# Later places for the readers of fresh transfers, and a later start of the first merged second-layer products, in a hand-planned Mamba-2 and expert-mixture kernel

## The chip, the core and the metric

The kernel runs on one core of one Trainium2 chip. The metric is the device time of one execution in microseconds; the time given is the median of several runs. The core has a matrix engine (TensorE, "PE" in the profile, with "PEld" for its weight loads), VectorE ("DVE"), ScalarE ("ACT"), GpSimd ("POOL") and SyncE ("SP"), which here issues nearly all transfers. Each engine takes its own instructions in the order in which the program lists them and waits at semaphores for the others.

## What is computed

Two blocks follow each other, all in float32. The first is a Mamba-2 scan over 4 sequences of 768 positions with 8 heads of 32 channels and a state of 16:

```python
L = np.exp(cum[:, :, :, None] - cum[:, :, None, :]) * causal
CB = np.einsum('bhin,bhjn->bhij', Cc, Bc)
y_intra = np.einsum('bhij,bhjd->bhid', CB * L, xc)
y_inter = np.einsum('bhin,bhnd->bhid', Cc, state) * decay_to_i[:, :, :, None]
y[:, :, sl] = y_intra + y_inter
state = decay_full[:, :, None, None] * state + np.sum(Bx, axis=2)
```

Its output, laid out as 3072 tokens of 256 channels, goes through four dense experts of 1024 hidden units, weighted by normalised domain probabilities:

```python
p = domain_probs / (domain_probs.sum(-1, keepdims=True) + 1e-09)
for e in range(E):
    h = np.maximum(x @ w1[e], 0.0)
    out += p[:, e:e + 1] * (h @ w2[e])
```

## The kernel before

The tokens are cut into 24 chunks of 128. Five blocks of chunk pairs are worked through, three of one scheme (`B`, two pairs) and two of another (`H`, three pairs). Both schemes replace plain products of the expert layers by fewer products of sums: sums of weights (L960, on VectorE or GpSimd), sums of tokens (L979), sums of products (L896, L1045, L1198). One product is a function call with two matmul instructions of 128 by 256 (L869); the profile shows four records for it. The 16 hidden slices of 256 are taken in groups, and a group in a block is a *unit*. A unit's first-layer products end in a gate (L904: relu times the domain probability, on VectorE); its second-layer products continue sums that lie in SBUF between units.

Those sums explain three ScalarE lines. A sum of a second-layer house is kept in a tile `v`: it is *seeded* into a PSUM bank (L883, copy `bank<-v`), products are added to it, and it is copied out again (L1146 for both halves, L1149 for one half). L878 copies an intermediate first-layer sum out of a bank.

The Mamba part of later chunks is woven in between. For each chunk a transfer brings the token data (`xb<-in_xbc_dram`, L430, L432 and L434) and the decays (`ab<-acut_d`). ScalarE then masks the chunk (`ctm<-xb`, L469, two instructions), VectorE scans the decays (L493), TensorE makes the scores (L476), VectorE multiplies them (L793), and TensorE makes outputs and states (L815, L509). Stored sums of weights are written to DRAM once (`w_d<-w`, L965) and reloaded in later blocks (`w<-w_d`, L957). Finished blocks are written out by 32 small stores each (L1253).

The order in which everything stands is made before launch. TensorE's order is written by hand: `put` (L1281) spreads several lists of products evenly over each other, and for every unit the second-layer products of the unit before (`behind`) are spread over its first-layer products (`seq`):

```python
merged = put(behind, seq) if behind else seq
```

For the first unit (`u` is 0) `behind` holds three products that continue one house begun just before the loop (L1340).

All other engines get their order from a planner, `Plan.run` (L185). It walks through time with an assumed cost for each piece of work; an engine takes, among the pieces that are ready, the one that is wanted earliest (`latest`). A piece whose input is a transfer (`kb` is set) counts as ready only `MARGIN`, 2.0 us, after the planned landing (L214). The planner also hands out tiles and banks. Then the pieces are issued in the order of their planned starts, and each engine keeps that order, whenever the inputs really come.

Of the kernel before, what the change touches and what calls it, by code (L numbers as in the profile page):

```python
# [18 lines left out]
HOP = 0.06  # L19
# [6 lines left out]
SOFT = 1  # L26
ROUND = 0, 3, 2, 0, 4
RATE, MARGIN = 330.0, 2.0
AFTER = 1
HOLD = 6.0  # L30
NEAR, WORTH, FIRST = .3, 1.0, 25.0
# [4 lines left out]
BUSY, CALM = 200.0, 1.06  # L36
AHEAD = 3
SOON = 3
EASY = 40.0
HELD = ("x", "w"), (5, 8), (0, 7)  # L40
APART = (0, 7),
# [37 lines left out]
class Plan:  # L79
# [105 lines left out]
    def run(self, line, at, begin):  # L185
# [19 lines left out]
        while todo:  # L205
            e = min(t, key=lambda e: t[e])
            now = t[e]
            best, soon, near = None, None, None
            late = self.late = max(0.0, t["PE"] - line[head].nominal) if head < len(line) else 0.0
            for w in waiting[e]:  # L210
                if w.start is not None or e == "PE" and w.place != head:
                    continue
                ready = max([w.ready, w.after.nominal + late if w.after else 0.0] + [
                    n.end + (MARGIN if n.kb and e != "SP" else -n.lag if n.by == e == "PE" else HOP)  # L214
                    for n in w.needs])
                if len(w.on) > 1 and e == "POOL":
                    if max(ready, now) + w.on[e] > w.latest + late + SLACK or self.backlog(
                            waiting["DVE"], now, t["DVE"], w) < (BACK if now > EASY else 99):
                        continue
                rank = w.latest  # L220
                if e == "DVE" and w.two and self.port > now + 0.05:
                    rank += YIELD
                if best is not None and ready <= now and rank >= best[0]:
                    continue
                when, homes = self.homed(
                    w, max(now, ready, self.port if e == "POOL" and w.port else 0.0))
                if when is None:
                    continue
                if when <= now + 0.02:
                    if best is None or rank < best[0]:  # L230
                        if e == "DVE" and w.two:
                            when = max(when, self.port)
                        best = rank, w, when, homes
                else:
                    if e == "DVE" and when <= now + NEAR and now < FIRST and (near is None or rank < near[0]):
                        near = rank, when
                    if soon is None or when < soon:
                        soon = when
# [16 lines left out]
            _, w, when, homes = best  # L255
# [84 lines left out]
def kernel(  # L340
# [361 lines left out]
    now = 13.2  # L702
# [266 lines left out]
    def token_sums(k):  # L969
        Y, scheme = {}, blocks[k].scheme  # L970

        def get(x):
            return (yT[k, x[1]], lambda v, i=x[0]: v.t[:, i]) if isinstance(x, tuple) else (
                Y[x], lambda v: v.t)

        for r, x, y, sign in scheme.tokens:
            v = Y[r] = value("Y")
            (vx, ax), (vy, ay) = get(x), get(y)
            plan.add({"DVE": D256}, lambda e, v=v, vx=vx, ax=ax, vy=vy, ay=ay, sign=sign: (  # L979
                on(e).tensor_add if sign > 0 else on(e).tensor_sub)(v.t, ax(vx), ay(vy)),  # L980
                two=True, reads=[vx, vy], writes=[v])
        for r in {r for h in scheme.houses for r in h} - {"x", "w"}:
            tokens[k, r] = get(scheme.right.get(r, r))
# [169 lines left out]
    def second(k, groups, houses, held=(), more=()):  # L1153

        seq = []
        for house in houses:
            terms = [
                (r, weights[k, fbs, 2][0][r][0], lambda r=r, fbs=fbs: weights[k, fbs, 2][1](r), T[r])
                for r in house for fbs, T in groups if r in T]
            terms += [t for t in more if t[0] in house]  # L1160
            for only in reversed(house) if house in held and house in APART else (None,):
                if terms:
                    seq += visit(k, house, terms, house in held, only)
        return seq
# [116 lines left out]
    def put(*seqs):  # L1281

        n = [len(s) for s in seqs]
        keys = [((i + (.5 if len(seqs) == 1 else (j + .5) / len(seqs))) / n[j], j, i)
                for j, s in enumerate(seqs) for i in range(n[j])]
        return [seqs[j][i] for _, j, i in sorted(keys)]
# [24 lines left out]
    ones = [(two, {1: begun[two][2]}) for two in twos]  # L1311
    line.extend([*firsts[8:], *second(0, ones[:SOON], [(1, 2)])])
    for c in range(4):
        carry(c)
    units, last_made = [], {}
    for k, b in enumerate(blocks):
        n = E if b.scheme is B else NG
        lead = ROUND[k]
# [8 lines left out]
    def unit_weights(k, groups):  # L1327
        if groups is None:
            plain_weights(k, 0)
        for fbs in groups or ():  # L1330
            for l in (1, 2):
                if fbs in last_made.get(k - 1, ()):
                    weights[k, fbs, l] = weights[k - 1, fbs, l]
                else:
                    operands(k, blocks[k].scheme, fbs, l)
        if groups:
            last_made[k] = groups

    token_sums(0)
    behind = second(0, ones[SOON:], [(1, 2)])  # L1340

    early = [((3 * g + 1, 3 * g + 2, 3 * g + 3), l) for g in range(NG) for l in (1, 2)]
    ending, ends = None, []
    for u, (k, groups) in enumerate(units):
        b = blocks[k]
        of_block = [v for v, (q, _) in enumerate(units) if q == k]
        i = u - of_block[0]
        if AHEAD <= u + 1 < len(units):
            unit_weights(*units[u + 1])
        if i == 0 and k:  # L1350
            token_sums(k)
        if groups is None:
            gates.pop((k, 0), None)
            seq, h = [], {}
            for n in range(b.scheme.pairs):
                s, h[0, n] = plain_first(k, 0, n)
                seq += s
            plain = plain_terms(k, [0], h, b.scheme.plain)
        else:
            made = [threes_first(k, fbs) if b.scheme is H else twos_first(  # L1360
                k, fbs, begun.get(fbs) if k == 0 else None) for fbs in groups]
            seq = put(*[s for s, _ in made])
            right = twos_right if b.scheme is B else threes_right
        merged = put(behind, seq) if behind else seq
        ends.append(merged[-1])
        if ending is not None:
            leave(*ending, due=lambda n=u + AFTER: ends[min(n, len(ends) - 1)])
            ending = None
        for _ in range(EARLY.count(u)):
            operands("early", H, *early.pop(0), merged[0],  # L1370
                     lambda n=u + SOFT: ends[min(n, len(ends) - 1)])
        if groups is None:
            behind = second(k, *held, HELD if k == len(blocks) - 1 else (), plain)
        else:
            held = [(fbs, right(h)) for fbs, (_, h) in zip(groups, made)], b.scheme.houses
            for fbs, T in held[0]:
                if k == 0 and fbs in begun:
                    del T[1]
            plain_next = u + 1 < len(units) and units[u + 1][1] is None
            if plain_next:  # L1380
                held = held[0], LATE
            behind = [] if plain_next else second(k, *held)
        if u == of_block[-1] and k < len(blocks) - 1:
            ending = k, result(k)

        at = {}
        if k < len(blocks) - 1:
            for unit, x, what in PAIRS_AT[len(of_block) if k else 0, blocks[k + 1].scheme.pairs]:
                if unit != i:
                    continue  # L1390
                cs = [blocks[k + 1].first + 2 * int(p) + j for p in what[1:] for j in range(2)]
                mark = len(line)
                if what[0] == "s":
                    for c in cs:
                        fetch(c)
                        decays(c)
                    scores(cs)
                else:
                    outputs(cs)
                    for c in cs:  # L1400
                        carry(c)
                at.setdefault(x, []).extend(line[mark:])
                del line[mark:]
        for x, w in enumerate(merged):
            line.extend(at.get(x, []))
            line.append(w)
# [54 lines left out]
```

## Time and profile before

| what | value |
|---|---|
| median of 3 runs | 624.72 us (624.41 to 624.77) |
| profiled execution | 626.2 us |
| its span, first to last instruction | 624.4 us |
| granted TensorE clock | 0.999 |
| TensorE busy | 616.9 us, 99% |
| VectorE busy | 533.0 us, 85% |
| ScalarE busy | 274.5 us, 44% |
| GpSimd busy | 182.8 us, 29% |
| DMA traffic | 127.44 MB, mean 204 GB/s |

A row of the timeline gives the start, the length, the engine, the line, the operation with output and inputs, and the number of instructions merged into the row; in brackets stands the idle time of the engine just before it and what ended it. A row of the waits names who waited for whom, the total, the number of times and the longest, in microseconds. Times in the trace count from the first instruction.

### The profile page before, as it was taken

What the parts mean: (1) busy time and instruction counts of PE and PEld (TensorE: products, weight loads), DVE (VectorE), ACT (ScalarE), POOL (GpSimd) and SP (SyncE); (2) the same over time, 40 slices, a digit from 0 to 9 for tenths busy, and PEclk for the clock granted to TensorE, in tenths of its full rate; (3) what the DMA queues carried; (4) which work ended last, traced back from release to release, by engine and by line L of the source; (5) the groups of instructions that cost most, each with busy time, mean ns of one, the idle gap of its engine ahead of it and who ended that gap; (6) DMA issues with size and microseconds to landing.
All of it is one profiled execution on the core that took longest, in us unless ns stands there. A gap on an engine that the chain in (4) does not pass through costs nothing.

```text
span 624.4 us, 10261 instructions
## 1 busy us (share of the span) xinstructions
PE 616.9 (99%) x3427; PEld 526.3 (84%) x3427; DVE 533.0 (85%) x879; ACT 274.5 (44%) x582; POOL 182.8 (29%) x208
## 2 busy tenths in 40 slices
PE   9999999999999999999999999999999999999997
PEld 4788888888888888888888788888888888888886
DVE  6999999999968799879788899959797977869684
ACT  5453463423356334336533445445443334555441
POOL 5106775563437575444450001200000000000010
PEclk9999999999999999999999999999999999999999
DMA  7997569884799878389998838635232339643001
GB/s 260 330 336 250 193 226 315 263 265 116 229 354 306 268 246 278 68 287 330 317 333 273 287 69 294 189 115 182 59 101 60 84 66 299 216 137 110 0 2 50
DMA packets 112627, 127.44 MB, mean 204 GB/s; under 512 B 28980, under 2 KB 78144, under 8 KB 112576
## 3 DMA queue, kind: packets, MB, share of 16 engines
q1 hardware_dynamic: 112420, 126.74, 63.0%
q8 instruction: 27, 0.44, 0.3%
q14 instruction: 24, 0.20, 0.1%
q10 hardware_dynamic: 156, 0.06, 0.0%
HBM read 101.87 MB, written 24.89 MB: 203 GB/s over the span
## 4 chain that ended last, share of the span: by engine, by line
PE 96%; ACT 1%; DVE 1%; DMA 1%; issue 0%; SPq 0%; ACTq 0%; DVEq 0%
PE bank L869 89%; PE bank L476 2%; PE bank L509 2%; PE bank L815 1%; PE bank L647 1%; DMA xb<-in_xbc_dram 1%; PE bank L623 0%; DVE v L904 0%; ACT ctm L469 0%; DVE LT L493 0%; DVE v L896 0%; ACT bank L883 0%; ACT v L878 0%; SPq L432 0%; PE bank L1267 0%
## 5 line engine op out<-in xcount | busy, mean ns | idle before, releaser
L869 PE MATMUL bank<-v,w 128*128 128x256 f32 x1816 | 429.7, 380 | 1.0 <-ACT bank L883 0.6
L869 PEld LDWEIGHTS bank<-v,w 128*128 128x128 f32 x1816 | 342.7, 190 | 54.2 <-issue 2.4
L869 PE MATMUL bank<-Y,w 128*128 128x256 f32 x824 | 210.9, 379 | 1.3 <-ACT bank L883 1.3
L896 DVE TENSOR_TENSOR v<-v,v 128x512 f32<-128x512 f32 x262 | 192.0, 763 | 17.5 <-ACT v L878 15.1
L869 PEld LDWEIGHTS bank<-Y,w 128*128 128x128 f32 x824 | 156.2, 190 | 23.6 <-ACT bank L883 1.7
L883 ACT COPY bank<-v 128x512 f32<-128x512 f32 (+1 forms) x201 | 112.4, 571 | 70.6 <-DVE v L896 35.8
L904 DVE SCALAR_TENSOR_TENSOR v<-bank,gate 128x512 f32<-128x512 f32 x172 | 116.1, 682 | 28.2 <-PE bank L869 21.9
L960 POOL TENSOR_TENSOR w<-w,w 128x256 f32<-128x256 f32 x103 | 99.3, 986 | 34.2 <-PE bank L869 18.1
L878 ACT COPY v<-bank 128x512 f32<-128x512 f32 x112 | 65.4, 585 | 96.8 <-PE bank L869 96.3
L1146 ACT COPY v<-bank 128x512 f32<-128x512 f32 x106 | 62.1, 585 | 100.7 <-PE bank L869 99.6
L896 POOL TENSOR_TENSOR v<-v,v 128x512 f32<-128x512 f32 x18 | 25.0, 1396 | 245.4 <-DVE v L896 154.7
L493 DVE TENSOR_TENSOR_SCAN LT<-ab,ident 128x512 f32<-128x512 f32 x42 | 56.2, 1355 | 1.0 <-DMA ab<-acut_d 1.0
L896 DVE TENSOR_TENSOR v<-bank,v 128x512 f32<-128x512 f32 x40 | 27.4, 686 | 8.5 <-PE bank L869 7.6
L503 POOL TENSOR_TENSOR MT<-xb,LT 128x64 f32<-128x64 f32 (+1 forms) x28 | 18.0, 647 | 49.8 <-DVE LT L493 23.4
L778 POOL TENSOR_TENSOR cts<-ctm,dec 128x256 f32<-128x256 f32 x20 | 17.8, 893 | 49.3 <-DVE v L896 14.6
L1198 DVE TENSOR_TENSOR v<-v,v 128x256 f32<-128x256 f32 x54 | 21.9, 442 | 9.2 <-ACT v L1146 9.2
L793 DVE TENSOR_TENSOR MT<-bank,LT 128x512 f32<-128x512 f32 x44 | 27.2, 678 | 1.1 <-PE bank L476 0.8
L1149 ACT COPY v<-bank 128x256 f32<-128x256 f32 x23 | 8.6, 373 | 38.0 <-PE bank L869 37.9
L960 POOL TENSOR_TENSOR w<-w 128x256 f32<-128x256 f32 x15 | 14.2, 951 | 30.8 <-DMA w<-in_w_dram 26.1
L469 ACT ACTIVATE ctm<-xb,tmask 128x128 f32<-128x128 f32 x48 | 16.6, 396 | 11.5 <-DMA xb<-in_xbc_dram 11.2
L1045 DVE TENSOR_TENSOR bank<-bank,v 128x512 f32<-128x512 f32 x24 | 16.6, 692 | 5.7 <-PE bank L869 5.6
L960 DVE TENSOR_TENSOR w<-w,w 128x256 f32<-128x256 f32 x35 | 15.6, 482 | 0.0
(73 smaller groups left out, 203.6 us busy)
## 6 DMA issues: line engine op xcount, KB each, us to landing
w<-w_d SPq DMA_DIRECT2D x138, 256.0 KB
w<-in_w_dram SPq DMA_DIRECT2D x126, 256.0 KB
w_d<-w SPq DMA_DIRECT2D x82, 256.0 KB
ab<-acut_d SPq DMA_DIRECT2D x21, 512.0 KB
w<-in_w_dram SPq DMA_DIRECT2D x42, 128.0 KB
gate<-p_d SPq DMA_DIRECT2D x10, 384.0 KB
xb<-in_xbc_dram SPq DMA_DIRECT2D x17, 192.0 KB
gate<-p_d SPq DMA_DIRECT2D x11, 256.0 KB
```

Source lines behind the costliest of these rows:

```text
L493: nc.vector.tensor_tensor_scan(out=LT.rearrange("p h s -> p (h s)")[:, lo:lo + w], data0=src, data1=ident.rearrange("p h s -> p (h s)")[:, ...
L503: nc.gpsimd.tensor_mul(MT[:, to, P:], b[:, h:h + n], LT[:, to, P - 1:P].to_broadcast([P, n, N]))
L778: plan.add({"POOL": .72}, lambda e: nc.gpsimd.tensor_mul(s["cts"].t, s["ctm"].t, s["dec"].t.unsqueeze(1).to_broadcast([HN, NT, P])), reads ...
L793: nc.vector.tensor_mul(s["MT"].t[:, js, h, 0:P], g, s["LT"].t[:, js, h])
L869: nc.tensor.matmul(out=o, lhsT=w[:, j], rhs=x if half is None else x[:, j], start=(start and j == 0), stop=(j == 1), skip_group_check=True)
L878: act(.5, lambda e: nc.scalar.copy(out=flat(v), in_=bank.t), reads=[bank], writes=[v])
L883: act(.54 if to - lo > FB else .32, lambda e: nc.scalar.copy(out=bank.t[:, lo:to], in_=flat(v)[:, lo:to]), reads=[v], writes=[bank])
L896: plan.add(engines, lambda e: (on(e).tensor_add if sign > 0 else on(e).tensor_sub)(flat(v), whole(x), whole(y)), reads=[x, y], writes=[v], ...
L904: dve(D512, lambda e: nc.vector.scalar_tensor_tensor(out=h.t, in0=whole(x).rearrange("p (j m) -> p j m", j=JJ), scalar=0.0, in1=g.t[:, 2 * ...
L960: plan.add({"POOL": .72} if due else B256, lambda e, r=r, x=x, y=y, sign=sign: (on(e).tensor_add if sign > 0 else on(e).tensor_sub)(view(r ...
L1146: act(.5, lambda e: nc.scalar.copy(out=flat(v), in_=bank.t), reads=[bank], writes=[v])
L1198: plan.add(engines, lambda e: (on(e).tensor_add if sign > 0 else on(e).tensor_sub)(o[1](), x[1](), y[1]()), reads=[v for v in vs if v is n ...
```

## The change

Two things change, both in the making of the order; no instruction's work changes. First, the planner has a second margin. From 100 us of planned time on, a piece on any engine but SyncE that reads a transfer counts as ready 6.0 us after the planned landing, unless its latest start lies less than 8 us ahead; then, and before 100 us, the 2.0 us stay. Second, in the first unit the first two first-layer products are taken out of the spreading and put ahead of it, so that the three merged second-layer products begin later.

```diff
 RATE, MARGIN = 330.0, 2.0
+LEEWAY, SURE = 6.0, 100.0
...
 SOON = 3
+BARE = 2
...
                 ready = max([w.ready, w.after.nominal + late if w.after else 0.0] + [
-                    n.end + (MARGIN if n.kb and e != "SP" else -n.lag if n.by == e == "PE" else HOP)
+                    n.end + ((MARGIN if now < SURE or w.latest + late < now + 8 else LEEWAY) if n.kb and e != "SP" else -n.lag if n.by == e == "PE" else HOP)
                     for n in w.needs])
...
-        merged = put(behind, seq) if behind else seq
+        lead = 0 if u else BARE
+        merged = seq[:lead] + put(behind, seq[lead:]) if behind else seq
```

Since the planner solves the whole order again, tiles, banks and the order on ScalarE, VectorE, GpSimd and SyncE shift throughout; in TensorE's order the three merged products of the first unit stand behind one more product each and nothing else moves. Line numbers after the change are mostly two higher (L871 for L869).

## The prediction

> **What bounds the kernel now.** I read the page first. TensorE is busy for 99% of the span at a granted clock of 0.999, and the chain that ended last is 96% TensorE, so all waits together are worth little; the question is which of TensorE's few waits the change removes, and which it makes.
>
> ```profile
> span 624.4 us, 10261 instructions
> PE 616.9 (99%) x3427; PEld 526.3 (84%) x3427; DVE 533.0 (85%) x879; ACT 274.5 (44%) x582; POOL 182.8 (29%) x208
> PE 96%; ACT 1%; DVE 1%; DMA 1%; issue 0%; SPq 0%; ACTq 0%; DVEq 0%
> 415.73 199.63 PE bank L869 x924
> ```
>
> The last line is from the chain in order of time: 924 matmul records without a break in 199.63 us, so 0.216 us each and 0.864 us for a product of four. That is the yardstick: a product is late by what its start lies behind the last product's start plus 0.864. Second, the waits of TensorE and, in the list of all waits, ScalarE's on fresh transfers:
>
> ```profile
> PE bank L869 <- ACT bank L883: 1.9, 2, 1.3
> ACT ctm L469 <- DMA xb<-in_xbc_dram: 11.2, 6, 2.9
> ```
>
> Third, the timelines at the two waits on the seed copies (L883). At 343 us (SyncE, ScalarE, TensorE):
>
> ```profile
> 339.62 0.84 SPq L432 DMA_DIRECT2D xb<-in_xbc_dram  x2
> 343.92 0.69 ACT L469 ACTIVATE ctm<-xb,tmask 128x128 f32<-128x128 f32 x2 [2.53 <-DMA xb<-in_xbc_dram]
> 344.52 0.56 ACT L1146 COPY v<-bank 128x512 f32<-128x512 f32 x1
> 344.98 0.59 ACT L883 COPY bank<-v 128x512 f32<-128x512 f32 x1
> 343.29 1.03 PE L869 MATMUL bank<-v,w 128*128 128x256 f32 x4
> 345.62 1.13 PE L869 MATMUL bank<-Y,w 128*128 128x256 f32 x4 [1.30 <-ACT bank L883]
> ```
>
> ScalarE takes its instructions in order. It stood 2.53 us at a mask whose token chunk had not landed; behind the mask stood the copy and the seed that TensorE needed. At 30 us:
>
> ```profile
> 30.03 0.37 ACT L1149 COPY v<-bank 128x256 f32<-128x256 f32 x1 [2.56 <-PE bank L869]
> 30.30 1.11 ACT L883 COPY bank<-v 128x512 f32<-128x512 f32 x2
> 29.83 1.03 PE L869 MATMUL bank<-Y,w 128*128 128x256 f32 x4
> 31.47 1.13 PE L869 MATMUL bank<-v,w 128*128 128x256 f32 x4 [0.61 <-ACT bank L883]
> ```
>
> Here no transfer is involved: a merged second-layer product comes one product after the sum that it continues, and the copy out and the seed back take longer than that one product.
>
> **The readers of fresh transfers (first part).** Count and duration of every instruction stay; only the planner's order moves, from 100 us on, by 6.0 instead of 2.0 us after the estimated landing, unless the reader is urgent. In the changed order ten of the twelve chunk masks after 170 us stand 6 to 16 matmul instructions (0.43 us each) further behind their transfer; two near 247 us keep their place. At 343 us the two transfers keep their places in SyncE's queue, the masks come 10 instructions (4.3 us) later, and the copy and the seed now stand ahead of them. The seed's last input is a VectorE L896 that began at 340.72 and took 0.68, so the seed can end near 342.0; its product is due at 343.29 + 0.864 = 344.15. The wait is gone with 2.1 us to spare. Its price: start late by 345.62 - 344.15 = 1.47, and the product behind it started at 346.59, 0.97 later instead of 0.864, so 0.11 for refilling. Together 1.58 us. Late next on ScalarE is the mask itself, still ending near 344.6; behind it stands a copy (L1149) that ran at 345.50 before, so nobody waits. The masks' readers are the scores at 373.5 us, 29 us of cover; without cover this move would cost its 4.3 us.
>
> One row against a rule. Measured: the chain shows 3.77 us from that transfer's last issue, at 340.04, to its landing. The Trainium skill, DMA: Bandwidth & Descriptors, section Anatomy of one DMA, gives about 2.0 us fixed plus bytes over 436 GB/s, fitted for the GpSimd path. My estimate by it is 2.45 us for 192 KB, so 2 us of margin would suffice, the seed would come only some 0.15 us late, this part would be worth about 0.2 us, and the forecast would stand near 624.1. The sum goes by the row.
>
> The other movers: GpSimd's sums of early operands come up to 4 us later. GpSimd was busy 126.5 of the 245 us from 100 to 345 us, and these sums go to DRAM and are reloaded only for the last two blocks, after 338 us, so I cost this at nothing; without that cover a product would wait the 4 us.
>
> **The merged products (second part).** It acts on the first unit alone: three merged products each move behind one more product. TensorE's order changes in nothing else. The first of them is then due at 29.83 + 2 x 0.864 = 31.56, the seed ended at 31.41: the wait is gone with 0.1 us to spare. Price: 31.47 - 30.69 = 0.78, plus refill 32.43 - 31.47 - 0.86 = 0.10, so 0.88 us.
>
> What is late next is VectorE, which hardly idles until 54 us.
>
> ```profile
> 30.81 1.76 DVE L960 TENSOR_TENSOR w<-w,w 128x256 f32<-128x256 f32 x5
> 39.56 1.22 DVE L493 TENSOR_TENSOR_SCAN LT<-ab,ident 128x512 f32<-128x512 f32 x1
> 40.69 0.67 DVE L904 SCALAR_TENSOR_TENSOR v<-bank,gate 128x512 f32<-128x512 f32 x1
> ```
>
> That L904 held TensorE at 41.42; due was 41.14, so 0.28 plus 0.10 of refill. Its counterpart in the changed order stands after 15 weight sums of 0.335 (five in 1.67 us), two combines and four gates of 0.60 (three L904 in 1.86 us) and one scan of 1.14 (L493 to the next): from 30.81 that is 5.03 + 3.60 + 1.14 = 9.77, so 40.58, and its product starts near 40.65 where it was due at 40.20. So the second wait grows from 0.28 to 0.45, and TensorE stands 41.42 - 40.65 = 0.77 us ahead. One scan that stood before this gate now comes after it: VectorE's further work ends 41.37 - 40.58 = 0.79 earlier by the gate but 1.14 later by the scan, 0.35 behind. A combine that took 0.76 there (58.58 to 59.34) goes to GpSimd, so the gate that ended near 59.94 ends near 59.53; its product, 60.14 before, is due at 59.37. With refill this gives back 0.2. I take 0.55 for this part; bounds 0 (VectorE takes all) and 0.88 + 0.38 = 1.26 (both waits go).
>
> **What the trace doesn't show.** The plan is solved again, so the orders of all four other engines change: a third short wait of TensorE, at 112.76 on a score product of VectorE (L793), 0.30 with refill, may go, stay or grow. I take 0.15 off; bounds +0.3 and -0.6 (one more L896 of 0.60 ahead of it). New waits have no row. Between 50 and 615 us the present order has two, of 0.30 and 1.58; I allow one like the smaller, 0.3, bounds 0 and 1.9 (as many as now).
>
> **Sum.** 1.58 + 0.55 + 0.15 - 0.30 = 1.98 us. The profiled execution took 626.2 (span 624.4 and 1.8 around it), 1.5 above the median of the runs, 624.72; it should come to 624.2, and the median to 622.7.
>
> **Rivals.**
>
> No change: the waits go, but the new order brings its own of the present size. 1.58 + 0.55 - 1.88 leaves 0.25, so 624.5; with VectorE giving back nothing and only one wait of 1.58 it is 624.0. For it: 85% VectorE, two places above with 0.1 us to spare, and hundreds of moved instructions. Against it: the present order met 565 us with just two waits, and one of those came from a late transfer, of which there will be fewer. A change that doesn't do what it says (the mask at 343 us stays) would also land here, at 624.72 - 0.55 = 624.2; the changed order speaks against it.
>
> Slower: SyncE's queue. Two reloads of stored sums (L957), wanted by the products at 166.8 and 168.5 us, were issued near 141 to 143 us, ahead of the 32 output stores that fill SyncE from 144.5 to 160.2 us. In the changed order they stand behind these stores, and three stores of early sums (L965) stand among them. Issued at 160.2 as the first reload is now, they land by 164.0: a load issued at 161.24 ended GpSimd's wait at 165.00, 3.8 us. Wanted at 166.1 after 0.7 us of gains; 2.1 us to spare. SyncE's own waits bound what can eat that: L965 on GpSimd at most 2.6 us, on VectorE at most 6.1. At 2.6 the wait is 0.5 and the time 623.2; at 6.1 it is 4.0 plus 0.1, and the time 626.8. It decides beyond 5.3 us of holding: then 3.25 us are lost, and 1.98 less 3.25 is slower by over 0.2%. Against it: the stores also start 8 instructions (3.5 us) earlier in the changed order.
>
> Faster still: both early waits go and nothing new comes, 624.72 - 3.14 - 0.3 = 621.3 with all three terms at their bounds.
>
> **How the numbers follow.** Forecast, with the faster end: 0.60. No change: 0.23. Slower: 0.17. About 0.2% (1.25 us) is what a measurement of this kernel can tell from no change: below 623.47 is faster, above 625.97 slower. The range leaves out 0.05 below and 0.15 above: 621.6 to 626.2. The forecast's own range is 621.6 to 623.5.
>
> **What would show it.** Right: no TensorE wait on L883 near 343 us, the seed ahead of the two masks on ScalarE, the list's wait of ctm on xb far below 11.2 us; no wait at 31 us, one of about 0.45 near 40.6 us; the scores that start at 109.66 start about 0.6 earlier, the last matmul about 2 us. Wrong: a wait of L869 on a DMA near 165 us (the slower rival), waits on L904 between 41 and 62 us that eat the 0.77, or any new wait above 1 us after 100 us.

## The result, and the profile after

The changed kernel takes 623.86 us (median of 20 runs, 623.26 to 624.86) where the kernel before takes 624.98 us on the same chip (median of 20, 623.88 to 626.64). The ratio is 0.998, with a 95% interval of 0.9973 to 0.9987. So it is faster by 1.1 us, 0.2%: just under what I had called the least that can be told, and little more than half of the 2.0 us forecast. (The ranges of times and the ratios in this document leave out three executions, of 647, 1531 and 1666 us, that ran in a slow state.)

The profiled execution took 623.26 us, 2.36 of it outside the span; in the profile before, 1.8 of 626.2 lay outside. The page after, its span, its engines and the engines' shares of the chain that ended last:

```profile
span 620.9 us, 10264 instructions
PE 615.4 (99%) x3427; PEld 526.0 (85%) x3427; DVE 533.5 (86%) x882; ACT 275.5 (44%) x582; POOL 179.1 (29%) x205
PE 97%; DVE 1%; ACT 1%; issue 0%; DVEq 0%
```

The span is 3.5 us shorter, the time only 2.9. DMA has left the chain. The list of waits after has no row of ScalarE's mask on its transfer (11.2 us in six waits before). TensorE's waits in the main products are these three; none is on a seed:

```profile
PE bank L871 <- ACT v L880: 0.3, 1, 0.3
PE bank L871 <- DVE v L906: 0.2, 1, 0.2
PE bank L871 <- DVE MT L795: 0.2, 1, 0.2
```

The timeline after at the two places of the prediction, near 340 us (ScalarE, SyncE, TensorE) and near 30 us (ScalarE, TensorE):

```profile
339.40 0.59 ACT L1148 COPY v<-bank 128x512 f32<-128x512 f32 x1 [2.58 <-PE bank L871]
339.89 0.60 ACT L885 COPY bank<-v 128x512 f32<-128x512 f32 x1
340.41 1.29 ACT L471 ACTIVATE ctm<-xb,tmask 128x128 f32<-128x128 f32 x4
333.92 0.84 SPq L434 DMA_DIRECT2D xb<-in_xbc_dram  x2
342.60 1.03 PE L871 MATMUL bank<-Y,w 128*128 128x256 f32 x4
```

```profile
29.64 1.11 ACT L885 COPY bank<-v 128x512 f32<-128x512 f32 x2
29.18 1.89 PE L871 MATMUL bank<-Y,w 128*128 128x256 f32 x8
30.90 1.04 PE L871 MATMUL bank<-v,w 128*128 128x256 f32 x4
```

The seed stands ahead of the masks and ends 2.1 us before its product starts at 342.60; the four mask instructions run without any wait. That they don't wait has a second cause beside their later place: the last chunk's transfers, in the row at 333.92, were issued 5.7 us earlier than before (339.62), while TensorE was only 1.6 ahead. Near 30 us eight records (two products) follow each other, and the product on the seed follows them with no gap. Two places are new or larger, near 58.7 and 111.5 us:

```profile
57.33 1.28 DVE L906 SCALAR_TENSOR_TENSOR v<-bank,gate 128x512 f32<-128x512 f32 x2
58.66 1.56 PE L871 MATMUL bank<-v,w 128*128 128x256 f32 x6 [0.24 <-DVE v L906]
111.47 1.35 PE L871 MATMUL bank<-v,w 128*128 128x256 f32 x5 [0.21 <-DVE MT L795]
```

**Where the time went.** I subtract each TensorE start before from its counterpart after, and count the refill of about 0.1 us behind a wait with the wait. TensorE is 0.67 us ahead at the first product of the expert layers (start-up: 13.20 against 12.53 us). It gains 0.86 more at 31 us and 0.36 at 41; loses 0.48 at 58.7, gains 0.15 of it back at the scores near 64, loses 0.11 at 80, 0.15 at 111.5 and 0.12 at 131; gains 0.39 at 172 and 1.55 at 343. The 0.39 at 172 is not the change's: a later execution of the kernel before (e11) gains as much there over this first one. The last matmul starts 3.12 us earlier. From there to the end of the span it is 3.75 us, where it was 4.19. But 0.6 us of this comes back outside the span, and this before was among the slowest of its runs and this after the fastest of its own. So the experiments also compare distributions.

### The profile page after: what moved, and what is told of

The parts are those of the page before. It is cut to its first block, busy times and chain, and to the rows that moved or that the text cites. A ratio compares the mean times of both kernels' runs of the same rounds, so it can differ in the third digit from the quotient of the medians.

```text
span 620.9 us, 10264 instructions
## 1 busy us (share of the span) xinstructions
PE 615.4 (99%) x3427; PEld 526.0 (85%) x3427; DVE 533.5 (86%) x882; ACT 275.5 (44%) x582; POOL 179.1 (29%) x205
## 4 chain that ended last, share of the span: by engine, by line
PE 97%; DVE 1%; ACT 1%; issue 0%; DVEq 0%
PE bank L871 91%; PE bank L511 2%; PE bank L478 2%; PE bank L649 1%; PE bank L817 1%; PE bank L625 0%; DVE v L906 0%; DVE w L962 0%; DVE LT L495 0%; DVE MT L795 0%; ACT ctm L471 0%; DVE v L898 0%; PE bank L1269 0%; PE bank L617 0%; ACT A L521 0%
## 5 line engine op out<-in xcount | busy, mean ns | idle before, releaser
L871 PE MATMUL bank<-v,w 128*128 128x256 f32 x1816 | 429.5, 380 | 0.7 <-ACT v L880 0.3
L871 PEld LDWEIGHTS bank<-v,w 128*128 128x128 f32 x1816 | 342.7, 190 | 53.8 <-issue 4.0
L871 PE MATMUL bank<-Y,w 128*128 128x256 f32 x824 | 210.6, 379 | 0.0
L898 DVE TENSOR_TENSOR v<-v,v 128x512 f32<-128x512 f32 x258 | 188.9, 764 | 16.4 <-ACT v L880 15.2
L871 PEld LDWEIGHTS bank<-Y,w 128*128 128x128 f32 x824 | 156.3, 190 | 21.9 <-issue 0.6
L962 POOL TENSOR_TENSOR w<-w,w 128x256 f32<-128x256 f32 x100 | 95.1, 973 | 60.2 <-PE bank L871 23.1
L880 ACT COPY v<-bank 128x512 f32<-128x512 f32 x112 | 65.5, 586 | 95.7 <-PE bank L871 92.3
L898 POOL TENSOR_TENSOR v<-v,v 128x512 f32<-128x512 f32 x22 | 30.3, 1382 | 261.8 <-DVE v L898 157.6
L495 DVE TENSOR_TENSOR_SCAN LT<-ab,ident 128x512 f32<-128x512 f32 x42 | 54.5, 1317 | 0.4 <-DMA ab<-acut_d 0.4
L1200 DVE TENSOR_TENSOR v<-v,v 128x256 f32<-128x256 f32 x56 | 24.6, 476 | 6.8 <-ACT v L1148 6.7
L505 POOL TENSOR_TENSOR MT<-xb,LT 128x64 f32<-128x64 f32 (+1 forms) x28 | 14.6, 529 | 36.9 <-DVE LT L495 29.7
```

Source lines behind the costliest of these rows:

```text
L495: nc.vector.tensor_tensor_scan(out=LT.rearrange("p h s -> p (h s)")[:, lo:lo + w], data0=src, data1=ident.rearrange("p h s -> p (h s)")[:, ...
L871: nc.tensor.matmul(out=o, lhsT=w[:, j], rhs=x if half is None else x[:, j], start=(start and j == 0), stop=(j == 1), skip_group_check=True)
L880: act(.5, lambda e: nc.scalar.copy(out=flat(v), in_=bank.t), reads=[bank], writes=[v])
L898: plan.add(engines, lambda e: (on(e).tensor_add if sign > 0 else on(e).tensor_sub)(flat(v), whole(x), whole(y)), reads=[x, y], writes=[v], ...
L962: plan.add({"POOL": .72} if due else B256, lambda e, r=r, x=x, y=y, sign=sign: (on(e).tensor_add if sign > 0 else on(e).tensor_sub)(view(r ...
L1200: plan.add(engines, lambda e: (on(e).tensor_add if sign > 0 else on(e).tensor_sub)(o[1](), x[1](), y[1]()), reads=[v for v in vs if v is n ...
```

## Experiments

"First to last product" is the time between the start of the first expert product and that of the last matmul in a profile; it leaves the start-up and the end aside. It is 607.02 us before, 604.58 after.

**Round one: the parts by themselves.** Three theories of the first part: its gain is a wait of steady length at 343 us (S); the wait varies with the landing of the token chunk (V); or the plan that is solved again matters more than the two parts (P).

e1 takes the kernel before and moves one thing in the finished order. `late` lists the chunk masks and GpSimd's readers of them (the lines that fill it are left out); its last four are those of the last two chunks:

```diff
...
+    last = late[-4:]
+    at = done.index(last[-1]) + 1
+    seeds = [i for i in range(at, len(done)) if done[i].by == "ACT"][:2]
+    rest = [w for w in done[:seeds[-1] + 1] if w not in last]
+    done = rest + sorted(last, key=lambda w: w.start) + done[seeds[-1] + 1:]
```

> The kernel before with one edit: on ScalarE the copy and the seed (L1146, L883) that stood behind the last two chunk masks at 343 us now stand ahead of them; every other engine's order is the same. Theory S (steady wait): the wait of 1.58 us at 343 us is there in every execution, so the time falls by 1.4 to 1.6 us. Theory V (varying landing): the profiled execution of before, 626.2 against a median of 624.98 in 20 runs, had a late landing; the wait is smaller or absent in most executions, so the median falls by 0.2 to 0.8 us. Both: no TensorE wait near 343 us in this trace.

Measured: 624.11 us (12 runs, 623.58 to 626.17) against 625.07 (29 runs, 623.33 to 627.03); ratio 0.9989, interval 0.9978 to 1.0. No wait near 343 us, first to last product 604.48. The masks of these two chunks are worth 0.7 us by the ratio (its interval reaches from nothing to 1.4) and 1.0 by the medians, not the 1.58 of the first trace. The scatter stays, though by one execution of the twelve, which took 626.17 us; the others lie within 1.0.

e2 is the first part alone (`BARE = 0`).

> The first part of the change alone (6.0 us margin from 100 us on, merged products as before). Theory S: -1.4 to -1.6 us, the early waits at 31 and 41 us stay at 0.88 and 0.38. Theory V: -0.2 to -0.8 us. Theory P (the plan that comes out of solving again counts more than the parts): a new wait above 0.5 us somewhere, so 0 or slower.

Measured: 623.26 us (12 runs, 622.71 to 623.51), ratio 0.9972 (0.9962 to 0.9981). The waits at 31 us (0.77) and 41 us (0.27) are there as before; first to last product 604.78. Its median lies below both kernels', and its times lie within 0.8 us of each other. It was not run beside the changed kernel, and the intervals of the two ratios overlap (0.9962 to 0.9981, 0.9973 to 0.9987); but the two ranges of times share only 0.25 us (622.71 to 623.51, 623.26 to 624.86).

e3 is the second part alone (`LEEWAY = 2.0`).

> The second part alone (merged products of the first unit two later, margin 2.0 throughout). Theory S: -0.5 us, with the wait of about 1.5 us near 343 us still there. Theory V: -0.3 to -0.8 us, and the wait near 343 us of another size than 1.47 in this trace. Theory P: the changed order makes waits elsewhere, 0 or slower.

Measured: 624.61 us (12 runs, 623.37 to 628.88), ratio 1.0005 (0.9986 to 1.0024): nothing. In its profile 2.36 us lie outside the span, as after the full change. TensorE starts late by 0.41 at 59.3 us, 0.18 at 111.9, 0.35 at 210.0 and 1.06 at 344.6.

e4 and e11 are the kernel before, profiled again; e11 was run last, but belongs here.

> The kernel before, unchanged, for a second trace. Theory S: a start 1.4 to 1.5 us late near 343 us again. Theory V: another size, 0 to 1.0 us, in an execution of about 625.0. Both: the waits at 31 and 41 us as before, since no transfer takes part in them.

> The kernel before, profiled a third time. If the wait at 343 us is set by when the token chunk happens to land, it has yet another length between 0.2 and 1.5 us (it was 1.47 and 0.27), while the waits at 31 and 41 us, where no transfer is involved, are the same to 0.05 us. If the first trace was a freak, it is again below 0.3.

e4 took 624.53 us. The chain of waits of its last blocks, and the timeline after it:

```profile
338.55 3.60 DMA xb<-in_xbc_dram
342.25 0.69 ACT L469 ACTIVATE ctm<-xb,tmask 128x128 f32<-128x128 f32 x2 [2.15 <-DMA xb<-in_xbc_dram]
343.32 0.59 ACT L883 COPY bank<-v 128x512 f32<-128x512 f32 x1
343.96 1.13 PE L869 MATMUL bank<-Y,w 128*128 128x256 f32 x4
```

The transfer takes 3.60 us, much as the 3.77 of the first trace, but was issued 1.5 us earlier (338.55 against 340.04), while TensorE was only 0.46 ahead. Its product starts 0.27 late, not 1.47. SyncE's order is the same in e1 and e7 below, and there and in e11 this last issue came at 337.57, 339.04 and 340.77 us: 3.2 us between the earliest and the latest of five executions. e11 took 626.18 us, as the first profile did, and lost its time elsewhere. Its timeline near 212 us, VectorE and then TensorE, and one line of its chain:

```profile
210.04 0.42 DVE L775 TENSOR_TENSOR_SCAN dec<-ah,zeros 128x128 f32<-128x128 f32 x1 [3.10 <-DMA ah<-ac_d]
210.39 0.67 DVE L904 SCALAR_TENSOR_TENSOR v<-bank,gate 128x512 f32<-128x512 f32 x1
213.51 0.89 DVE L775 TENSOR_TENSOR_SCAN dec<-ah,zeros 128x128 f32<-128x128 f32 x1 [1.85 <-DMA ah<-ac_d]
214.32 0.66 DVE L904 SCALAR_TENSOR_TENSOR v<-bank,gate 128x512 f32<-128x512 f32 x1
211.20 1.97 PE L869 MATMUL bank<-v,w 128*128 128x256 f32 x8 [0.74 <-DVE v L904]
215.03 1.13 PE L869 MATMUL bank<-v,w 128*128 128x256 f32 x4 [0.80 <-DVE v L904]
206.45 6.97 DMA ah<-ac_d
```

A decay scan on VectorE (L775) is also a reader of a fresh transfer. It stands ahead of a gate, TensorE needs the gate, and the small transfer took 6.97 us. That is not rare: the same transfer took 6.2 us in the first trace (issued at 205.07, the scan's wait ended at 211.26) and 6.4 in e4 (204.14, 210.51). In e11 it was above all issued later, at 206.45, as the token chunk was in the first trace. TensorE loses 0.9 us twice; at 343 us, already that late, it has no visible wait at all. So V holds, though by the issue more than by the transit, with a second place that I had not seen: first to last product is 607.02, 605.36 and 607.01 us in three executions of one program. In three of the changed order (the first, e5 and e6 below) it is 604.58, 604.52 and 604.53. The third length that I expected at 343 us did not show; the loss had moved. The waits at 31 and 41 us were the same each time, 0.77 and 0.27.

In the order after, these scans run unhindered (the timeline after, VectorE):

```profile
207.44 0.73 DVE L777 TENSOR_TENSOR_SCAN dec<-ah,zeros 128x128 f32<-128x128 f32 x2
209.09 0.59 DVE L777 TENSOR_TENSOR_SCAN dec<-ah,zeros 128x128 f32<-128x128 f32 x1
209.61 0.66 DVE L906 SCALAR_TENSOR_TENSOR v<-bank,gate 128x512 f32<-128x512 f32 x1
```

**Round two: why both parts together are slower than the first alone.** Theory N: the second part's gain is given back by VectorE inside the span. Theory L: time is lost outside the span, where GpSimd's instruction stream is loaded once more at the end. The trace shows loads of 8 KB of instructions on a queue of their own, without the engine that they are for. In the profile after, the last of them starts at 622.3 us, 1.4 after the span's end, and in e3 two start 1.6 and 2.2 after it; in e2 the last starts at 581.5 us. By the program, GpSimd has 330 instructions before, 324 after, 340 in e2 and 323 in e3 (the traces have one fewer of each).

e5 is the changed kernel once more; e6 is the same with

```diff
+    pad = const.tile([P, 1], FP32, name="pad")
+    for _ in range(16):
+        nc.gpsimd.memset(pad, 0.0)
```

at the end, which makes GpSimd's stream as long as that of e2.

> The changed kernel, unchanged, beside the next three and for a second trace. Theory N (the second part's gain of 0.8 us at 31 to 41 us is given back inside the span by VectorE's gates and score products): time near 623.9; waits near 58.7 and 111.5 us as in the first trace, time outside the span 2.4. Theory L (the second part loses 0.6 us outside the span, because GpSimd's shorter instruction stream, 324 instead of 340 with the first part alone, ends where its last piece must be loaded at the very end): the same time, 2.4 us outside the span, and an instruction load after the end of the span.

> The changed kernel with 16 one-element memsets of a tile of their own behind all of GpSimd's work, so that GpSimd's stream has 340 instructions; GpSimd does nothing else in the last 250 us. Theory L: 1.8 us outside the span, the last instruction load before the end, 0.6 us faster than the changed kernel, 623.2 or a little below. Theory N: no change against it, 623.9.

e5: 623.89 us (623.34 to 624.38), 0.9984 (0.9973 to 0.9996); first to last product 604.52; outside the span 2.37. e6: 623.55 us (623.07 to 623.63), 0.9978 (0.9968 to 0.9989); 604.53; outside 2.11, the last load of 8 KB at 595.8 us. That the load at the end was GpSimd's follows from this pair, which differs in GpSimd's stream alone. Sixteen instructions of no use make the kernel 0.34 us faster at the median, half of what L expected. The intervals overlap. e2 and the kernel before have 1.8 outside, so another 0.3 is not explained by L.

e7 is e1 with ten such instructions, to see the same at the end of the other order.

> The kernel before with the last two chunk masks behind the copy and the seed, as in the first experiment, and 10 such memsets. Theory L: 3.75 instead of 4.17 us from TensorE's last instruction to the end of the span, so 0.4 faster than without them, 623.6 to 623.7. Theory N: as without them, 624.1.

Measured: 623.41 us (622.67 to 625.66), ratio 0.9977 (0.9962 to 0.9993). From the last matmul to the span's end it takes 3.76 us instead of the 4.17 of e1. First to last product is 604.88, 0.40 longer than in e1, because its first product starts 0.41 earlier and this is eaten by 22 us; the last matmul starts at 617.68 in both. In e1 GpSimd's closing drain instruction starts 0.37 us after the semaphore instruction before it and takes 0.23; in e7 it is 0.08 and 0.08. These are the 0.4 us. The last load starts just behind the span's end in e1 (621.91 against 621.85) and at 595.6 in e7; so the drain did not wait for that load's data, and by what the two are tied is open. What the pair shows is that ten more instructions on GpSimd take 0.4 us off the end. With the first part GpSimd has them, so 0.4 us of its gain is the length of GpSimd's stream.

e7 also bounds what is left for the other readers: with these masks moved and the stream at 340 it has 0.9977, 1.4 us less than before; the whole first part (e2) has 0.9972, 1.75 us. The other readers add 0.3 us by the ratios, 0.15 by the medians, which is less than either interval; what sets e2 apart is its scatter, 0.8 us against 3.0.

e8 gives the 6.0 us to readers on ScalarE alone (`MARGIN if e != "ACT" or ...`), e12 to all but these (`MARGIN if e == "ACT" or ...`), both without the second part and with GpSimd's stream at 340.

> The first part for ScalarE's readers alone (the chunk masks), VectorE's and GpSimd's readers with 2.0 us as before; 9 memsets make GpSimd's stream 340 long as with the first part alone. If the gain of the first part is the masks: as the first part alone, 623.1 to 623.5, no wait above 0.3 us near 343 us. If the other readers' places count too: 0.3 us or more above that.

> The first part for every reader of a transfer except those on ScalarE, without the second part, GpSimd's instruction stream at 340 instructions. In this order the three decay scans (L777, VectorE) near 210 us stand 18 to 22 products behind their transfers where they stood 7 to 11 in the order of before; the chunk masks on ScalarE stay 5 to 16 products behind theirs. Theory (the kernel before loses a varying time at two places, at the decay scans near 210 us and at the masks near 343 us): no wait of VectorE on ah near 210 us, ScalarE still waits on xb, by 3 to 11 us in all; the highest of its times lies below 625.5 where the kernel before reaches 626 and more, and the median is 623.3 to 624.2. Rival (only the masks matter, 210 us was a freak of one execution): the median is 624.5 to 625.0 and the times scatter over 3 us as those of before do.

e8: 623.49 us (622.91 to 623.98), 0.9974 (0.9962 to 0.9987). e12: 623.26 us (11 runs, 622.69 to 624.13), 0.9971 (0.9956 to 0.9986). Each half gives nearly all. This was my first error with e8: I took the gain to be the masks'. e12 tells why neither separates them: in its order too the seed stands ahead of the late mask (its timeline, ScalarE), since the plan is solved anew.

```profile
340.35 0.60 ACT L885 COPY bank<-v 128x512 f32<-128x512 f32 x1
342.24 0.69 ACT L471 ACTIVATE ctm<-xb,tmask 128x128 f32<-128x128 f32 x2 [1.29 <-DMA xb<-in_xbc_dram]
```

The mask still waits, and nobody behind it is in a hurry. At another place of e12 somebody is: at 304 us a mask waits 4.83 us for its transfer, a copy behind it (L880) ends at 306.06, and TensorE's product starts at 306.12, 0.23 late. In e8 the scan still waited 0.9 us at 211.5, but no gate stands right behind it, and TensorE lost nothing there. What the runs do show is the scatter. Where either place keeps an urgent step behind a reader, times spread by 2.6 us (e1), 3.0 (e7), 5.5 (e3) and 3.5 to 5.8 (before, beside the experiments); in e2, e5, e6, e9 and e10 by 0.6 to 1.0, in e8 and e12 by 1.1 and 1.4, and by 1.6 in the first 20 runs of the changed kernel, beside 2.8 in as many of the kernel before. The sets have 6 to 35 runs, a range grows with their number, and in e1 it is one run that makes it; so this is a pattern, not a proof.

**Round three: what eats the lead of the second part.** Compare TensorE's starts in e6 with those in e2, again with the refills. It is 0.84 us ahead behind 31 us and 1.21 behind 41. It gives back 0.49 at the gate near 59, of which 0.15 return at the scores near 64, then 0.07 at 80, 0.48 at 112 and 0.11 at 131; 0.21 are left at the end. If VectorE takes it back, less work on VectorE must return it. e9 is e6, e10 is e2, both with

```diff
-                dve(1.15, lambda e, lo=half * part: scan(
+                dve(1.15, lambda e, lo=half * part: None if c == 5 else scan(
```

> The changed kernel with GpSimd's instruction stream at 340 instructions (as in e6), and the two decay scans of chunk 5 (L495, VectorE, 1.14 us each, planned between 42 and 50 us) left out, so that this chunk's decays are stale; the order of everything else is the same. Theory (VectorE, which does not idle from 42 to 100 us, takes back the 0.9 to 1.1 us that the later merged products win): VectorE is 2.3 us ahead behind the scans, the wait on the gate L906 near 58.7 (0.3 to 0.41) goes, those on L795 near 111.5 and 131 shrink by about 0.5 together, and first to last product takes 603.8 to 604.1 us where it took 604.5; the time is 622.7 to 623.2. Rival (the lead is given back by other things than VectorE): first to last product stays at 604.5 and the time at 623.5.

> The first part alone (as in e2) with the same two scans of chunk 5 left out. Without the later merged products TensorE has no lead that VectorE could take back: only the wait of 0.27 near 41.4 lies ahead of the scans and stays, so first to last product stays at 604.6 to 604.8 and the time at 623.2 to 623.3. Rival (less VectorE work is worth the same with and without the second part, so it has nothing to do with the lead): first to last product falls by as much as in e9.

e9: 622.44 us (6 runs, 622.06 to 622.73), 0.9966 (0.9953 to 0.9979). e10: 623.21 us (12 runs, 622.84 to 623.62), 0.9973 (0.9957 to 0.9988), as e2. VectorE from 42 to 62 us in e6 and then in e9 (the stretch, its length, VectorE's busy time and instructions, granted clock, DMA's share and GB/s), and VectorE and TensorE at the gate in e6, then in e9:

```profile
42.00:62.00 20.00, 20.00 (x30) 1.00 0.75 235
```

```profile
42.00:62.00 20.00, 19.00 (x30) 1.00 0.87 284
```

```profile
57.98 1.28 DVE L906 SCALAR_TENSOR_TENSOR v<-bank,gate 128x512 f32<-128x512 f32 x2
59.31 1.99 PE L871 MATMUL bank<-v,w 128*128 128x256 f32 x8 [0.25 <-DVE v L906]
```

```profile
57.87 0.69 DVE L906 SCALAR_TENSOR_TENSOR v<-bank,gate 128x512 f32<-128x512 f32 x1 [0.45 <-PE bank L871]
57.60 3.19 PE L871 MATMUL bank<-v,w 128*128 128x256 f32 x14
```

In e6 VectorE has not a tenth of a microsecond to spare in these 20 us, and TensorE waits for its gate. In e9 VectorE waits for TensorE at the gate, and the matmuls run on. First to last product falls by 0.63, from 604.53 to 603.90: TensorE gains 0.41 at this gate, 0.11 just behind it and 0.12 at the scores near 64 us, and nothing anywhere else. In e10, with the same scans left out and no lead to protect, TensorE gains nothing up to 62 us and 0.31 at the scores near 64; its first to last product is longer, 605.26, because at 22 us, ahead of the scans, it lost 0.79: the 0.36 by which it had started earlier, and 0.43 more. So the gate's 0.5 us belong to the lead, which settles N there; the gain at the scores does not, and the medians of e2 and e10 don't show it. Of the medians' 1.1 us between e6 and e9, 0.4 in the profiles is an earlier first product, a matter of the start-up, and 0.3 lies outside the span; that is why the time came out below the 622.7 to 623.2 that I expected. The wait at 111 us did not shrink as I expected: it stayed 0.37, so it does not come from the work before 60 us. Nor can it, by the trace of e6: there VectorE itself waits for TensorE, 0.89 us before 100.37 and 0.37 before 104.68. Its lag is gone by then, and the wait at 112 arises in the row of work without a gap that it has from 104.68 to the score products at 110.76. This row is another in e2, so by these traces the loss there comes from the order of the new plan and not from the lead handed on; no run separates the two.

## Why the prediction was right, and where it was not

The sign held, the measured 623.86 lies in the stated range, and both mechanisms are in the traces: the seed ahead of the masks at 343 us with 2.1 us to spare, no wait at 31 us. But that range, 621.6 to 626.2, takes in the rivals too. The forecast's own range ended at 623.5, and 623.86 lies beyond it, in the stretch from 623.47 on that I had called no change; that the gain can be told at all is owed to 20 runs of each. The forecast of 622.7 was 1.2 us too low. By its steps:

**The first part, 1.58 us.** The mechanism was right; the term was the stall of one execution (1.47 and 0.11 of refill). Other executions of the same program lost 0.27 there, or nothing. e1, which does only this, gained 0.7 to 1.0, with an interval from 0 to 1.4. The two transfers did not keep their places in SyncE's queue, as I had said: in the changed kernel the last was issued 5.7 us earlier, at 334.33. With the 3.77 us of the first trace I estimate its landing at 338.1, ahead of the copy at 339.40, so the masks would hardly have held the seed in their old place either. The changed kernel alone can't tell the two; e1, where SyncE's order stays, shows what the masks' place does. The error is in how I went from the profile to the median: I took 626.2 less 1.98 and then subtracted the 1.5 us by which the profile lay above the median. But a good part of that 1.5 was the late landing that the change removes, so it was counted twice. Without the second subtraction the sum says 624.2, 0.3 above the 623.86 measured.

**Row or rule.** The rule of the Trainium skill, page DMA: Bandwidth & Descriptors, section Anatomy of one DMA, gave an estimate of 2.45 us for 192 KB. The issue that I timed carries only 96 KB, 96 rows of 1 KB (the 192 KB are the issue at 339.06); for these the same rule gives an estimate of 2.23 us. The second trace again shows 3.60 where the first showed 3.77, so the row was the better guide to the transit. But the transit was not what varied here: the issue was, by 1.5 us.

**The other movers, at nothing.** Here I looked at GpSimd's sums and passed over VectorE's decay scans near 210 us. The trace of before had only one wait there, 0.61 us, that cost TensorE nothing. In e11 it cost 1.9 us. The 0.4 us at the end of the kernel, which the prediction has no term for, are the larger part of why the first part alone gives 1.75 us by its ratio (0.28% of 625) although the masks give less than I said; for the scans and all other readers 0.3 us or less are left at the median, not told apart from nothing.

**The second part, 0.55 us.** The 0.88 at 31 us came (0.86 to 0.89). The second wait was to grow to 0.45 near 40.6 us; it went instead. VectorE in e6:

```profile
30.40 1.76 DVE L962 TENSOR_TENSOR w<-w,w 128x256 f32<-128x256 f32 x5
37.88 1.89 DVE L906 SCALAR_TENSOR_TENSOR v<-bank,gate 128x512 f32<-128x512 f32 x3
39.69 1.22 DVE L495 TENSOR_TENSOR_SCAN LT<-ab,ident 128x512 f32<-128x512 f32 x1
```

The scan behind the gates starts at 39.69, where my count of instructions had the fourth gate end at 40.58, 0.9 us later. I had counted 15 weight sums from 30.81 on; from the counterpart at 30.40 on the trace has 11, and four are 1.34 us, less 0.68 that VectorE idled. (The due time was off too: 41.14 less 0.88 is 40.26, not 40.20.) The lead behind 41 us was thus 1.2 instead of 0.77. The give-back at the gate near 59 us was forecast in its place and for its reason, VectorE without idle time, but as 0.2; it was 0.49, or 0.34 with what came back at the scores. Then waits on VectorE took 0.59 more at 112 and 131 us. The part left 0.2 to 0.3 us inside the span, and lost 0.6 outside it: on top of the first part it made the kernel slower, 623.26 to 623.89.

**The third wait, 0.15 off.** Wrong way: at 112 us it grew from 0.20 to 0.37, within the 0.6 that I had allowed for growth. In the kernel before it is no steady wait either: 0.20 in the first trace and in e11, 0.10 in e4, none in e1.

**New waits, 0.30.** Smaller: 0.11 at 131 us, already counted above.

**The slower rival** did not come near. The reloads were issued at 159.96 us, as supposed, and no product waited for them:

```profile
159.96 1.85 SPq L959 DMA_DIRECT2D w<-w_d  x4
```

**The no-change rival** was nearer than the forecast in its number, 624.0 to 624.5, but not by its mechanism: new waits did not take the place of the old ones. The gain was smaller, and part of it was lost outside the span.

**The faster end.** 3.14 already holds the third wait's 0.3; with all terms at their bounds the sum gives 621.6, not 621.3.

## What to carry to other kernels

A stall that ends with a transfer has a distribution; one trace shows one draw of it. Before pricing its removal, profile the same kernel two or three times, and do not subtract from the median what the profiled execution lost to that stall. Look at when the transfer is issued as well as at how long it takes: here the issue varied more. Look for every urgent step that stands behind a reader of a fresh transfer, also where this trace shows no loss: e2 makes the kernel steady to 0.8 us as well as faster, and its median lies below that of the full change, by leaving out the half whose lead is mostly lost again in waits on VectorE, and with which 0.6 us more lie outside the span.

## What the runs showed of the hardware

- One small transfer of decays (32 KB) took 6.2, 6.4 and 6.97 us from issue to landing in three executions; the last 96 KB of a token chunk took 3.6 and 3.8 us. What made SyncE issue the token chunk 1.5 us earlier in one execution than in another is open; the difference is there already at 330 us, where the reloads ahead of it (L957) were issued at 328.72 in e4, 330.76 in the first trace and 331.17 in e11.
- Instruction loads show at the end: with GpSimd's stream at 340 instructions instead of 330 or 324, the last load of 8 KB comes at 581 to 596 us instead of at or after the end. The span's last stretch is 0.4 us shorter (e1 to e7), or the time outside the span 0.26 us shorter (e5 to e6). Why the latter stayed at 2.1 us in e6 and was 1.8 in e9, with the same length, is open; e9 has two fewer instructions on VectorE.
- The first expert product starts at 13.17 to 13.21 us in most profiles and at 12.53 to 12.81 in five, with no change near it; 0.4 to 0.7 us of difference between two single profiles can be that alone, though in e7 and e10 it was gone by 22 us.
